# Block 0 of an FNet-plus-MLP kernel: centred rows go into its first product, and the tokens' scale is multiplied onto that product's sums

## The chip, the core and the metric

The kernel runs on one core of one Trainium2 chip. A core has five engines with a queue each: PE (TensorE, the matrix product), DVE (VectorE), ACT (ScalarE), POOL (GpSimd) and SP (SyncE, which here only starts transfers). Each takes its instructions strictly in its own order and waits on semaphores of the others. The metric is the device time of one execution in microseconds (us).

## What is computed

x has 2048 tokens of 640 numbers, float32. Each token is normalized over its 640 numbers, and three things are added up:

```
xn  = (x - mean(x)) / sqrt(var(x) + 1e-5)          # per token
A   = Real(DFT_tokens(DFT_hidden(xn)))              # by products with given cos/sin matrices
B   = gelu(xn @ w1 + b1) @ w2 + b2                  # 640 -> 1536 -> 640
out = x + A + B
```

The change touches the start of B. The normalization is two steps per token: subtract the mean ("centre") and multiply by one number r = 1/sqrt(var + 1e-5). As r belongs to a token and not to one of the 640 numbers, (x - mean) * r @ w1 is the same as r * ((x - mean) @ w1).

## The kernel before

**Tiles.** The tokens are worked in four blocks of 512. In a block, w1's 1536 columns are 12 units of 128. `hidden(g)` makes unit g's 128 x 512 sums in one bank of the accumulator: 15 matmuls of 128 x 512 (five slices of the 640 numbers, three matmuls each, because each operand is split into a high part, rounded to the type float32r in which the matmuls run, and a low remainder, and high*high, high*low and low*high are added). `gelu` copies the sums through the activation (`unit`), and splits the result into high (`high`, on ACT) and low (`low`, on DVE, source minus high). `output(i)` is another 15 matmuls with w2. `prep_w1` and `prep_w2` split the weights of a unit in the same manner, the high part on ACT, the low one on DVE. So the third matmul of each `hidden` needs a DVE result.

**Start.** Block 0's four row tiles (128 tokens each) are loaded, the PE is kept busy with `NWARM` matmuls on zeros, the rows are normalized into `xp`, turned with 20 PE transposes into five banks, and split from there into XT. The first loads of w1 go into the buffers that the warming matmuls read, so load 0 waits for the first `NGATE[0]` of these.

**Loop.** After units 0 and 1 comes `for i in range(10)`: split w1 of unit i+3 and w2 of unit i+1, run `hidden(i+2)`, its `gelu`, then `output(i)`. The order of each engine's work is the order of the program text; nothing reorders it. Woven into it are the jobs of `background(i)` (ahead of `hidden`) and `late(i)` (behind `gelu`): blocks 1 ("a", tokens 512 to 1023) and 2 ("b", tokens 1024 to 1535) are loaded, their statistics taken (`ln_stats`), they are normalized in place, and copied by DMA into another layout, `put_z`: `Z["b"]` (z_b in the profile, from the rows `r`) and `Z["a"]` (named row in the profile, from the rows `rt`); 16 transfers of 80 KB each, b's half on POOL's and half on SP's queue, a's all on POOL's. `put_rows` writes normalized rows to a scratch tensor `xn`. From z_b and z_a, `make_forms` makes transposed and split operands that the next stage needs: a DVE transpose into one of two buffers, then high on ACT and low on DVE. Forms b (vb0, vb1, ob0) are made in `background(4)`, forms a (ua0, ua1, va0, then an addition onto z_b) in `background(6)`.

The functions and lines that matter below: `split`/`high`/`low` L176 to L189, `load_x` L208, `ln_stats` L215, `ln_scale` L222, `ln_apply` L231, `transpose_z` L259, `load_w1` L278, `product` L300 to L302, `hidden` L320, `unit` L340, `add` L463, the warming matmuls L666, `transpose_x` L682, block 0's normalization L690 to L734, `put_z` L762, `put_rows` L770.

## Time and profile before

| what | value |
|---|---|
| runs shown | 851.45, 851.50 and 852.02 us, median 851.5 |
| profiled execution: span from first to last instruction | 849.9 us |
| its own time | not listed; the runs' median is 1.6 us above the span |
| PE busy | 841.9 us, 99% of the span |
| DVE, ACT, POOL busy | 686.7, 368.6, 67.7 us |
| DMA | 166.5 MB, mean 196 GB/s |

In the rows of a timeline stand the start in us from the span's start, the length, the engine, the line, the operation, what is written and read by the program's names, the shape and count, and in brackets how long the engine stood idle before and what ended that. "x15" is a merged run of 15 instructions. The profile's names drop buffer numbers: `ab` is a unit's activation, `hs` its split, `xab`, `as` and `w1f` are places of split w1 (and later of forms), `xc`, `r`, `rt` of split w2. In the rows of a tile's view stand line, engine, operation, count, shortest/median/longest in ns, and first and last start in us.

### The profile page before, as it was taken

The numbers are of one execution on the slowest core, as the hardware profiler recorded it, in microseconds if no ns is written. First come the engines' busy times: TensorE is split into PE (matmuls) and PEld (weight loads), VectorE is DVE, ScalarE is ACT, GpSimd is POOL, SyncE is SP. The second block draws the span as 40 slices with busy tenths as digits, with TensorE's granted clock in tenths as the row PEclk, the third lists the DMA queues.
The fourth block names the chain that finished last, engine by engine and source line by source line (L and its number), as shares of the span: only waits on it lengthen the run. The fifth ranks groups of instructions, "written<-read, shape, count | busy, mean of one in ns | idle before, by whom it ended". The sixth has DMA issues, their size and how long they took to land.

```text
span 849.9 us, 10599 instructions
## 1 busy us (share of the span) xinstructions
PE 841.9 (99%) x3711; PEld 696.7 (82%) x3711; DVE 686.7 (81%) x909; ACT 368.6 (43%) x527; POOL 67.7 (8%) x116
## 2 busy tenths in 40 slices
PE   8999999999999999999999999999999999999997
PEld 7888888888888888888888888888888888888886
DVE  7979889767844778979978887889967998885687
ACT  7655666654453555443444344232323433323241
POOL 0440024222301000000000000000000000000002
PEclk9999999999999999999999999999999999999999
DMA  8995667878977897958744679763745799705464
GB/s 230 288 248 158 139 163 250 260 223 305 262 192 199 333 323 138 209 120 193 158 137 107 167 220 283 165 144 99 214 150 156 229 237 234 303 19 180 124 172 108
DMA packets 199141, 166.53 MB, mean 196 GB/s; under 512 B 61648, under 2 KB 170192, under 8 KB 198576
## 3 DMA queue, kind: packets, MB, share of 16 engines
q1 hardware_dynamic: 188320, 140.42, 62.7%
q0 software_dynamic: 7600, 24.91, 8.7%
q10 hardware_dynamic: 3168, 0.52, 0.3%
q8 instruction: 29, 0.48, 0.2%
q14 instruction: 24, 0.20, 0.1%
HBM read 115.75 MB, written 46.14 MB: 190 GB/s over the span
## 4 chain that ended last, share of the span: by engine, by line
PE 98%; DMA 1%; DVE 0%; ACT 0%; SPq 0%; issue 0%; ACTq 0%
PE banks L301 29%; PE banks L302 29%; PE banks L300 29%; PE banks L320 10%; DMA row<-in_A_x_dram 1%; PE banks L682 0%; DVE st L215 0%; ACT xp L714 0%; SPq L208 0%; DVE yo L1722 0%; DVE mv L216 0%; ACT mv L707 0%; DVE mv L708 0%; ACTq L707 0%
## 5 line engine op out<-in xcount | busy, mean ns | idle before, releaser
L186 ACT ACTIVATE as<-r 128x1024 fp32r<-128x1024 f32 x80 | 85.0, 1062 | 171.1 <-PE banks L302 150.4
L300 PE MATMUL banks<-as,xab 128*128 128x512 f32 x407 | 158.3, 389 | 0.0
L302 PE MATMUL banks<-as,xab 128*128 128x512 f32 x407 | 158.3, 389 | 0.0
L301 PE MATMUL banks<-as,xab 128*128 128x512 f32 x407 | 158.3, 389 | 0.0
L189 DVE TENSOR_TENSOR as<-r,as 128x1024 fp32r<-128x1024 f32 x80 | 97.2, 1215 | 38.1 <-ACT as L186 38.0
L301 PEld LDWEIGHTS banks<-as,xab 128*128 128x128 f32 x407 | 76.4, 188 | 15.9
L302 PEld LDWEIGHTS banks<-as,xab 128*128 128x128 f32 x407 | 76.4, 188 | 15.8
L300 PEld LDWEIGHTS banks<-as,xab 128*128 128x128 f32 x407 | 76.4, 188 | 15.8
L300 PE MATMUL banks<-as,xc 128*128 128x512 f32 x224 | 87.1, 389 | 0.0
L301 PE MATMUL banks<-as,xc 128*128 128x512 f32 x224 | 87.1, 389 | 0.0
L302 PE MATMUL banks<-as,xc 128*128 128x512 f32 x224 | 87.1, 389 | 0.0
L186 ACT ACTIVATE as<-rt 128x1024 fp32r<-128x1024 f32 x32 | 34.0, 1063 | 72.5 <-PE banks L302 57.9
L320 PE MATMUL banks<-xt,xab 128*128 128x512 f32 x240 | 56.8, 390 | 0.0
L189 DVE TENSOR_TENSOR hs<-ab,hs 128x512 fp32r<-128x512 f32 x36 | 24.7, 685 | 37.6 <-ACT hs L186 37.6
L320 PEld LDWEIGHTS banks<-xt,xab 128*128 128x128 f32 x240 | 45.0, 188 | 9.4
L301 PEld LDWEIGHTS banks<-as,xc 128*128 128x128 f32 x224 | 42.1, 188 | 8.8
L302 PEld LDWEIGHTS banks<-as,xc 128*128 128x128 f32 x224 | 42.0, 188 | 8.7
L300 PEld LDWEIGHTS banks<-as,xc 128*128 128x128 f32 x224 | 42.1, 188 | 8.7
L1280 POOL DMA_DIRECT2D out_dram<-u x4 | 2.6, 658 | 568.8 <-DVE u L463 568.8
L302 PE MATMUL banks<-hs,xc 128*128 128x512 f32 x120 | 46.7, 389 | 0.0
L300 PE MATMUL banks<-hs,xc 128*128 128x512 f32 x120 | 46.7, 389 | 0.0
L301 PE MATMUL banks<-hs,xc 128*128 128x512 f32 x120 | 46.7, 389 | 0.0
(240 smaller groups left out, 1678.9 us busy)
## 6 DMA issues: line engine op xcount, KB each, us to landing
raw<-in_A_dft_seq_re_dram SPq DMA_DIRECT2D x64, 256.0 KB, 5.4
raw<-in_A_dft_seq_im_dram SPq DMA_DIRECT2D x64, 256.0 KB, 5.1
w1r<-in_B_w_dram SPq DMA_DIRECT2D x144, 80.0 KB, 3.5
wit<-wst POOLq DMA_DIRECT2D x15, 384.0 KB, 4.2
wit<-wst POOLq DMA_DIRECT2D x20, 256.0 KB, 4.5
forms_ab<-xab SPq DMA_DIRECT2D x4, 1280.0 KB, 7.7
xab<-wit SPq DMA_DIRECT2D x13, 384.0 KB, 4.5
row<-xn SPq DMA_DIRECT2D x14, 320.0 KB, 5.3
```

The costliest lines, as they stand in the source:

```text
L186: nc.scalar.activation(h, s, AF.Copy)
L189: nc.vector.tensor_tensor(l, s, h.bitcast(F32), op=ALU.subtract)
L300: nc.tensor.matmul(acc, wh, mh, start=first, stop=False, skip_group_check=goes_on)
L301: nc.tensor.matmul(acc, wh, ml, start=False, stop=False, skip_group_check=goes_on)
L302: nc.tensor.matmul(acc, wl, mh, start=False, stop=last, skip_group_check=goes_on)
L320: nc.tensor.matmul(acc, W1[i][:, a, j * P : (j + 1) * P], XT[j][:, b], start=n == 0, stop=n == len(steps) - 1)
L1280: queues[q % len(queues)].dma_start(rows_of(out, t)[:, :, q * DQ + c0 : q * DQ + c1], src[q * B : (q + 1) * B])
```

## The change

1. **Start.** Rows 0 to 3 are only centred, not scaled (`centre` on DVE, `centre_beside` on ACT): rows 0 and 2 and most of 3 on DVE, row 1 and two slices of row 3 on ACT. Variances of rows 1 and 3 come from a squared sum on ACT (`spread_beside`), row 3's only after XT is split. The high part of w1's unit 0 moves from ACT to DVE. The order of unit 0's matmuls (`FIRST`) changes a little, its last one runs amid unit 1's. 14 warming matmuls instead of 19; the first load of w1 waits for 6 of them instead of 7.
2. **Scale.** r of the 512 tokens is computed after the split of XT (square root on ACT, four small steps on DVE), spread over 128 partitions by four PE transposes amid `hidden(1)`, and copied into `scale`. Each of the 12 units of block 0 gets one more DVE instruction: sums times `scale` (128 x 512), ahead of its activation.
3. **Rows of block 0** are no longer normalized in place on DVE (four instructions, L231) but on ACT from `xp` (`rows_beside(0)`).
4. **Blocks 1 and 2.** Block 2's rows are normalized on ACT (`ln_apply_beside`) at step 1; block 1 gets its own table of statistics `MVA`, its statistics and its normalization move to step 2 (they were taken at step 2 and ended at step 3), on DVE. Square roots are issued ahead of a unit's activation (`roots`), with an extra small square root before them.
5. **Order.** The low parts of the weights (DVE) are issued after the unit's multiplication, inside `gelu`. Forms b move from `background(4)`, ahead of `hidden(6)`'s activation, to `late(3)`, behind `hidden(5)`'s: in DVE's order they stood behind w1's unit 7, and stand ahead of it now, with unit 6's multiplication in between. Forms a move from step 6 to step 5: they stood behind w1's unit 9 and stand ahead of it now, with unit 8's multiplication in between. From step 4 on `background` runs behind `gelu`. The transfers of each queue keep their order.

```diff
-NWARM = 19
-NGATE = (7, 10)
+NWARM = 14
+NGATE = (6, 9)
...
-        low(l, s, h)
+        if rest is None:
+            low(l, s, h)
+        else:
+            rest.append(lambda: low(l, s, h))
...
-        m = MV[:, :n]
-        ve, r, t = m[:, :, 2], m[:, :, 3], m[:, :, 4]
-        nc.scalar.activation(r, m[:, :, 1], AF.Sqrt, bias=eps[:, 0:1])
-        nc.vector.tensor_scalar(ve, m[:, :, 1], EPS, None, op0=ALU.add)
+    def roots(m):
+        nc.scalar.activation(m[:, :, 3], m[:, :, 1], AF.Sqrt, bias=eps[:, 0:1])
...
+        m = (MVA if 4 <= c < 8 else MV)[:, slot[c]]
         eng.tensor_scalar(xt[c], xt[c], m[:, 0:1], m[:, 3:4], op0=ALU.subtract, op1=ALU.mult)
+    def ln_shift():
+        nc.vector.scalar_tensor_tensor(MV[:, :, 5], MV[:, :, 0], -1.0, MV[:, :, 3], op0=ALU.mult, op1=ALU.mult)
+    def ln_apply_beside(c):
+        m = (MVA if 4 <= c < 8 else MV)[:, slot[c]]
+        nc.scalar.activation(xt[c], xt[c], AF.Identity, bias=m[:, 5:6], scale=m[:, 3:4])
...
             acc = a
+        if g < NF:
+            add(a, acc, scale, ALU.mult)
+            acc = a
         nc.scalar.activation(a, acc, AF.Gelu_apprx_tanh, bias=b1c[:, i : i + 1])
...
-    FIRST = [(0, 0), (0, 2), (1, 0), (1, 2), (0, 1), (2, 0), (2, 2), (1, 1), (3, 0), (3, 2)]
-    FIRST += [(2, 1), (4, 0), (4, 2), (3, 1), (4, 1)]
+    FIRST = [(0, 0), (1, 0), (0, 2), (1, 2), (2, 0), (2, 2), (0, 1), (3, 0), (3, 2), (1, 1)]
+    FIRST += [(4, 0), (4, 2), (2, 1), (3, 1), (4, 1)]
...
-    last = 1
-    f, m = MV[:, 0], MV[:, last]
...
+    def centre(c, j0=0, j1=ND):
+        nc.vector.tensor_scalar(
+            chunked(xp[:, c])[:, :, j0:j1],
+            xt[c].rearrange("p (q c i) -> p q c i", q=Q, i=B)[:, :, j0:j1],
+            MV[:, c, 0:1],
+            None,
+            op0=ALU.subtract,
+        )
+    def centre_beside(c, j0=0, j1=ND):
+        nc.scalar.activation(
+            chunked(xp[:, c])[:, :, j0:j1],
+            xt[c].rearrange("p (q c i) -> p q c i", q=Q, i=B)[:, :, j0:j1],
+            AF.Identity,
+            bias=MV[:, c, 5:6],
+        )
+    scratch = mr.tile([P, 2 * TB], F32, tag="hs", bufs=3, name="scratch")[:, :D]
+    def mean_beside(c):
+        nc.scalar.activation(scratch, xt[c], AF.Copy, scale=-1.0 / D, accum_out=MV[:, c, 5:6])
+    def spread_beside(c):
+        nc.scalar.activation(scratch, xp[:, c], AF.Square, scale=D**-0.5, accum_out=MV[:, c, 1:2])
-    nc.scalar.activation(W1[0][:, 0], first_w1, AF.Copy)
+    centre(0)
+    mean_beside(1)
+    centre_beside(1)
+    spread_beside(1)
+    ln_stats(2)
+    centre(2, 0, 2)
+    mean_beside(3)
+    centre(2, 2, ND)
+    nc.vector.tensor_scalar(MV[:, 3, 0:1], MV[:, 3, 5:6], -1.0, None, op0=ALU.mult)
+    centre_beside(3, 0, 2)
+    centre(3, 2, ND)
     transpose_x(0, 0, ND)
+    transpose_x(1, 0, ND)
     transpose_x(2, 0, 2)
     transpose_x(3, 0, 2)
-    transpose_x(last, 0, ND)
     transpose_x(2, 2, ND)
-    transpose_x(3, 2, ND - 1)
+    transpose_x(3, 2, ND)
+    W1[0], first_w1 = slots[1, 0], w1r.pop(0).rearrange("p a b -> p (a b)")
+    nc.vector.tensor_copy(W1[0][:, 0], first_w1)
     nc.vector.tensor_tensor(W1[0][:, 1], first_w1, W1[0][:, 0].bitcast(F32), op=ALU.subtract)
     for j in range(ND):
         split(XT[j][:, 0], XT[j][:, 1], tacc[j])
-        if j == 0:
-            hidden(0, slice(0, 1))
-            transpose_x(3, ND - 1, ND)
...
     A["rows_a"] = rows_in("rt2")
     for c in range(NC, 2 * NC):
         load_x(c, home=A["rows_a"])
-    acc0 = hidden(0, slice(1, None))
+    acc0 = hidden(0, slice(0, 14))
     prep_w1(1)
-    acc1 = hidden(1)
+    spread_beside(3)
+    v, r, t = MV[:, :, 1], MV[:, :, 3], MV[:, :, 4]
+    nc.scalar.activation(r, v, AF.Sqrt, bias=eps[:, 0:1])
+    nc.vector.reciprocal(r, r)
+    nc.vector.scalar_tensor_tensor(t, r, -0.5, r, op0=ALU.mult, op1=ALU.mult)
+    nc.vector.scalar_tensor_tensor(t, v, EPS, t, op0=ALU.add, op1=ALU.mult)
+    nc.vector.scalar_tensor_tensor(r, t, 1.5, r, op0=ALU.add, op1=ALU.mult)
+    prep_w1(2)
     prep_w2(0)
-    prep_w1(2)
+    acc1 = hidden(1, slice(0, 2))
+    hidden(0, slice(14, None))
+    hidden(1, slice(2, 6))
+    for c in range(NC):
+        nc.tensor.transpose(bank(0)[:, c * P : (c + 1) * P], MV[:, c, 3:4].to_broadcast([P, P]), ident)
+    hidden(1, slice(6, None))
+    scale = rows.tile([P, TB], F32, tag="yt", bufs=2, name="scale")
+    nc.scalar.activation(scale, bank(0), AF.Copy)
     load_w2(3)
     load_w1(5)
...
                 xn[:, t * B : (t + 1) * B].rearrange("(c a) r d -> a r c d", a=NC)[a], rows[a * B : (a + 1) * B]
             )
-    def background(i):
+    def rows_beside(i):
         if i == 0:
             for c in range(NC):
-                ln_apply(c)
+                nc.scalar.activation(
+                    row_places[:, c].rearrange("p (q c i) -> p q c i", q=Q, i=B),
+                    chunked(xp[:, c]),
+                    AF.Copy,
+                    scale=MV[:, c, 3:4],
+                )
             put_rows(0, row_places)
+        if i in (1, 2):
+            nc.scalar.activation(eps[:, 1:2], eps[:, 0:1], AF.Sqrt)
+    def background(i):
+        if i == 0:
             ln_stats(8)
             ln_stats(9)
         if i == 1:
             ln_stats(11)
+            roots(MV)
         if i == 2:
-            ln_stats(4)
-            ln_stats(5)
-        if i == 4:
-            open_place(*PLACES[7])
-            new_forms(0, "vb", "ua", "va")
-            make_forms("b", "vb0", "vb1", "ob0")
-        if i == 6:
+            for c in range(NC, 2 * NC):
+                ln_stats(c)
+            roots(MVA)
+        if i == 5:
             put_rows(1, A["rows_a"], nc.sync)
             new_forms(3, "t1")
             make_forms("a", "ua0", "ua1", "va0")
-        if i >= 6:
+        if i >= 5:
             (ua, va), (ub, vb) = ((Z[k][:, :, : 2 * B], Z[k][:, :, 2 * B : 4 * B]) for k in "ab")
+        if i == 5:
+            add(ub, ub, ua, ALU.subtract)
         if i == 6:
-            add(ub, ub, ua, ALU.subtract)
-        if i == 7:
             make_forms("a", "oa0", "va1")
             open_place(*PLACES[8])
+        if i == 7:
             make_forms("b", "t10", "t11")
         if i == 8:
+            add(ua, vb, ua, ALU.subtract)
+            add(va, va, vb, ALU.subtract)
+        if i == 7:
             add(vb, vb, ub, ALU.subtract)
             turn_x("t20", "b")
             turn_x("t21", "b")
-            add(ua, vb, ua, ALU.subtract)
-            add(va, va, vb, ALU.subtract)
+        if i == 9:
             load_xo(0)
             for q in range(Q):
...
     def late(i):
+        if i == 3:
+            open_place(*PLACES[7])
+            new_forms(0, "vb", "ua", "va")
+            make_forms("b", "vb0", "vb1", "ob0")
         if i == 0:
             ln_stats(10)
+    def beside_split(i, lows):
         if i == 1:
-            ln_scale(NC)
+            ln_scale_table(MV)
+            ln_shift()
+        for f in lows:
+            f()
+        if i == 1:
             Z["b"] = zo_tile("z_b")
             for c in range(2 * NC, 3 * NC):
-                ln_apply(c)
+                ln_apply_beside(c)
             put_z(Z["b"], A["rows_b"], nc.gpsimd, nc.sync)
             put_rows(2, A["rows_b"])
         if i == 2:
-            ln_stats(6)
-            ln_stats(7)
-    def normalize_a():
-        ln_scale(NC)
-        Z["a"] = as_z(row_places)
-        for c in range(NC, 2 * NC):
-            ln_apply(c)
-        put_z(Z["a"], A["rows_a"], nc.gpsimd)
+            ln_scale_table(MVA)
+            Z["a"] = as_z(row_places)
+            for c in range(NC, 2 * NC):
+                ln_apply(c)
+            put_z(Z["a"], A["rows_a"], nc.gpsimd)
     XF = {}
...
             form(2)
-    gelu(0, acc0)
-    gelu(1, acc1)
+    a0 = unit(0, acc0)
+    a1 = mr.tile([P, TB], F32, tag="ab", bufs=2, name="ab1")
+    def second(k):
+        if k:
+            add(a1, acc1, scale, ALU.mult)
+    split_unit(0, a0, second)
+    nc.scalar.activation(a1, a1, AF.Gelu_apprx_tanh, bias=b1c[:, 1:2])
+    split_unit(1, a1)
     for i in range(NF - 2):
-        prep_w1(i + 3)
-        if i == 3:
-            normalize_a()
+        lows = []
+        prep_w1(i + 3, rest=lows)
         if i == NF - 3:
             new_pieces()
             make_pieces(0, "Ah", "Al")
-        prep_w2(i + 1)
+        prep_w2(i + 1, lows)
+        rows_beside(i)
+        if i < 4:
+            background(i)
+        acc = hidden(i + 2)
+        if i == NF - 3:
+            more_forms()
+        gelu(i + 2, acc, lambda k: beside_split(i, lows) if k else None)
         if i + 6 < NF + 3:
             load_w1(i + 6)
         load_w2(i + 4)
-        background(i)
-        acc = hidden(i + 2)
-        if i == NF - 3:
-            more_forms()
-        gelu(i + 2, acc)
+        if i >= 4:
+            background(i)
         late(i)
         output(i)
     prep_w2(NF - 1)
```

More of the change, by code (lines that the diff above doesn't have):

```diff
@@ L133 @@
     ident = early.tile([P, P], F32, name="ident")
+    MVA = early.tile([P, 4, 6], F32, name="mva")
     es_r = ExitStack()
@@ L174, in chunked, with split @@
         return ap.rearrange("p (c q i) -> p q c i", q=Q, i=B)
-    def split(hi, lo, src, perm=False):
+    def split(hi, lo, src, perm=False, rest=None):
         h, l, s = (hi, lo, src)
@@ L210, in ln_stats @@
     def ln_stats(c):
-        m = MV
+        m = MVA if 4 <= c < 8 else MV
         st = ST[c % 2]
@@ L682, in transpose_x @@
             nc.tensor.transpose(tacc[j][:, c * P : (c + 1) * P], xp[:, c, j * P : (j + 1) * P], ident)
-    last = 1
-    f, m = MV[:, 0], MV[:, last]
-    root, step, shift = f[:, 3:4], f[:, 4:5], f[:, 5:6]
-    ln_stats(0)
-    nc.scalar.activation(root, f[:, 1:2], AF.Sqrt, bias=eps[:, 0:1])
-    scratch = mr.tile([P, 2 * TB], F32, tag="hs", bufs=3, name="scratch")[:, :D]
-    nc.scalar.activation(scratch, xt[last], AF.Copy, scale=-1.0 / D, accum_out=m[:, 5:6])
-    nc.scalar.activation(
-        chunked(xp[:, last]),
-        xt[last].rearrange("p (q c i) -> p q c i", q=Q, i=B),
-        AF.Identity,
-        bias=m[:, 5:6],
-    )
@@ L699 @@
-    nc.scalar.activation(scratch, xp[:, last], AF.Square, scale=D**-0.5, accum_out=m[:, 1:2])
-    nc.vector.reciprocal(root, root)
-    nc.vector.scalar_tensor_tensor(step, root, -0.5, root, op0=ALU.mult, op1=ALU.mult)
-    nc.vector.scalar_tensor_tensor(step, f[:, 1:2], EPS, step, op0=ALU.add, op1=ALU.mult)
-    for c in (2, 3):
-        ln_stats(c)
-    others = MV[:, 1:NC]
-    v, r, t = others[:, :, 1], others[:, :, 3], others[:, :, 4]
-    nc.scalar.activation(r, v, AF.Sqrt, bias=eps[:, 0:1])
@@ L721 @@
-    nc.scalar.activation(xp[:, last], xp[:, last], AF.Copy, scale=m[:, 3:4])
-    W1[0], first_w1 = slots[1, 0], w1r.pop(0).rearrange("p a b -> p (a b)")
-    nc.scalar.activation(W1[0][:, 0], first_w1, AF.Copy)
-    for j0, j1 in ((0, 2), (2, ND)):
-        for c in (2, 3):
-            ln_apply_chunked(xp[:, c], c, j0, j1)
+    def centre(c, j0=0, j1=ND):
[6 more added lines that the diff above has]
+        )
@@ L1098, in between @@
         if p == 3:
-            ln_scale(NC)
+            roots(MV)
+            ln_scale_table(MV)
             Z["z"] = zo_tile("z3")
```

34 lines of the change are left out of this document (10 added, 24 removed).

## The prediction

> **What bounds the kernel now.** I read the page, the PE's waits, then each engine's timeline from 0 to 70 us.
>
> ```profile
> span 849.9 us, 10599 instructions
> PE 841.9 (99%) x3711; PEld 696.7 (82%) x3711; DVE 686.7 (81%) x909; ACT 368.6 (43%) x527; POOL 67.7 (8%) x116
> ```
>
> ```profile
> PE banks L666 <- DVE warm L657: 1.9, 1, 1.9
> PE banks L682 <- ACT xp L714: 0.7, 1, 0.7
> ```
>
> ```profile
> 1.92 7.05 PE L666 MATMUL banks<-warm 128*128 128x512 f32 x19 [1.92 <-DVE warm L657]
> 9.71 2.27 PE L682 MATMUL banks<-ident,xp 128*128 128x128 f32 x19 [0.73 <-ACT xp L714]
> 11.73 0.48 PE L320 MATMUL banks<-xt,xab 128*128 128x512 f32 x1
> 12.07 10.32 PE L320 MATMUL banks<-xt,xab 128*128 128x512 f32 x44
> 22.23 0.39 PE L300 MATMUL banks<-hs,xc 128*128 128x512 f32 x1
> 46.03 3.56 PE L320 MATMUL banks<-xt,xab 128*128 128x512 f32 x15
> ...
> 52.83 3.56 PE L320 MATMUL banks<-xt,xab 128*128 128x512 f32 x15
> ...
> 66.43 3.56 PE L320 MATMUL banks<-xt,as 128*128 128x512 f32 x15
> ```
>
> PE waits only in the first 10 us; from 12.07 on it never does. A step of the loop, 30 matmuls, takes 6.80 (from 46.03, hidden(6), to 52.83, hidden(7)), so one takes 0.227. So time is won only by an earlier first product, and lost wherever something behind it comes late. That PE never waits says nothing about margin; the other queues do.
>
> **The start.** What the change touches there:
>
> ```profile
> 3.73 0.89 DVE L215 BATCH_NORM_STATS2 st<-row 128x6 f32<-128x320 f32 x2 [1.20 <-DMA row<-in_A_x_dram]
> ...
> 6.23 0.89 DVE L215 BATCH_NORM_STATS2 st<-row 128x6 f32<-128x320 f32 x2 [0.46 <-DMA row<-in_A_x_dram]
> ...
> 11.83 3.07 DVE L189 TENSOR_TENSOR xt<-banks,xt 128x512 fp32r<-128x512 f32 x5
> ```
>
> ```profile
> 5.10 0.72 ACT L692 ACTIVATE scratch<-row 128x640 f32<-128x640 f32 x1
> ...
> 5.95 0.83 ACT L693 ACTIVATE xp<-row,mv 128x640 f32<-128x640 f32 x1
> 6.81 0.74 ACT L699 ACTIVATE scratch<-xp 128x640 f32<-128x640 f32 x1
> ...
> 8.66 0.90 ACT L714 ACTIVATE xp<-row,mv 128x640 f32<-128x640 f32 x1
> ...
> 11.03 2.56 ACT L186 ACTIVATE xt<-banks 128x512 fp32r<-128x512 f32 x5
> ```
>
> Five warming matmuls fewer, at the warm 0.23, end that run at 8.97 - 1.15 = 7.8. Row 0 is centred long before (statistics from 3.73, DVE), row 1 too. Row 3's chain is ACT's: mean of row 1 (0.85 to the next), centring (0.86), squares (0.93), mean of row 3 (0.85), two slices centred (about 0.4): 3.9 us from row 1's landing, which lies between 3.73 and 5.10; from 4.6 (my estimate) to 8.5. Twenty transposes at 0.12 (2.27/19) from 7.8 end at 10.1, row 3's first about 9.1. ACT's five splits follow each 0.51 (2.56/5) from 9.3; DVE's five lows each 0.61 (3.07/5) from 10.1, behind w1's parts. First product 10.0, one gap of 0.25 for the second split, 45 matmuls at 0.227 = 10.2, four added transposes 0.48: output(0) at 20.9 against 22.23. Gain 1.35; if row 1 lands at 3.73 or 5.10, 1.5 or 0.8. The new root and its DVE steps (0.93 + 0.3 on ACT, 4 x 0.2 on DVE) end near 14.8, as the PE reaches the added transposes at 15: bounds 0 and 0.5, taken as 0. Hidden(7) would begin at 52.83 - 1.35 = 51.5.
>
> **Steps 0 to 2.** Every unit gets a DVE multiplication from the accumulator, some 0.6 us like the lows from banks. DVE loses the rows of block 0 and of block 2, which ACT gains.
>
> ```profile
> 22.53 2.17 DVE L231 TENSOR_SCALAR row<-row,mv 128x640 f32<-128x640 f32 x4
> 24.62 0.88 DVE L215 BATCH_NORM_STATS2 st<-r 128x6 f32<-128x320 f32 x2
> ...
> 25.65 0.83 DVE L215 BATCH_NORM_STATS2 st<-r 128x6 f32<-128x320 f32 x2
> ```
>
> Units 0 and 1: the scale's copy ends near 16.2, the activation's load 17.5, activation, high and low of unit 0 follow by 19.6, and output(0) asks at 20.9: covered by 1.3. Step 0: ACT is through unit 1 at 20.2, splits two weights (1.4) and makes four rows of block 0 (0.8 each, by L693 and L714), to 24.8; DVE had them at 24.70 (22.53 + 2.17), so POOL's transfers of them start as before. They delay unit 2's activation to 24.8 and its high to 26.0, which output(2) needs only at 34.5. Step 1: DVE, from 26.0, has a low, two statistics (1.03 each, 24.62 to 25.65), a multiplication, five small steps and then unit 4's w1 low, done near 31.3; hidden(4)'s third matmul is due at 31.5. Step 2: a weight low (w2), unit 3's low, four statistics (4.1), a multiplication and unit 5's w1 low, near 38.1; due at 38.3. Margins of 0.2; I cost both at 0, with 0 to 1 as bounds. ACT pays two square-root loads and two activation loads, as many as before, plus two small roots at 0.2:
>
> ```profile
> 35.30 1.28 ACT L340 ACT_TABLE_LOAD   x1
> 36.60 0.69 ACT L340 ACTIVATE ab<-banks,b1c 128x512 f32<-128x512 f32 x1
> ```
>
> A switch costs 1.30 by these rows. The Trainium skill, "ScalarE: Activation LUTs", section "What ACT_TABLE_LOAD costs", adds a drain of about 1.38, 2.66 in all; here the next activation starts at once, so the trace does not agree. By it ACT, behind two switches, would have block 2 normalized 2.8 later, and z_b and the end of the kernel with it, near 856; I give that 0.01.
>
> **Forms b, where the sum is decided.**
>
> ```profile
> 33.05 2.18 DVE L231 TENSOR_SCALAR r<-r,mv 128x640 f32<-128x640 f32 x4
> ...
> 45.79 0.68 DVE L189 TENSOR_TENSOR hs<-ab,hs 128x512 fp32r<-128x512 f32 x1
> 46.39 0.81 DVE L189 TENSOR_TENSOR xab<-w1r,xab 128x640 fp32r<-128x640 f32 x1
> 47.12 0.82 DVE L189 TENSOR_TENSOR xc<-w2r,xc 128x640 fp32r<-128x640 f32 x1
> 49.94 1.30 DVE L259 STREAM_TRANSPOSE ztvb<-z_b 128x512 f32<-128x512 f32 x2 [2.00 <-DMA row<-rt]
> ...
> 53.49 0.69 DVE L189 TENSOR_TENSOR xab<-ztob,xab 128x512 fp32r<-128x512 f32 x1
> ...
> 62.69 1.30 DVE L259 STREAM_TRANSPOSE ztua<-row 128x512 f32<-128x512 f32 x2 [1.05 <-DMA row<-rt]
> ...
> 67.98 0.69 DVE L189 TENSOR_TENSOR hs<-ab,hs 128x512 fp32r<-128x512 f32 x1
> ```
>
> ```profile
> L762 POOL DMA_DIRECT2D z_b<-r x8: 552/552/553, 35.9 to 39.7; - x8
> L762 SPq DMA_DIRECT2D z_b<-r x8: 610/744/1512, 36.0 to 41.9; - x8
> ...
> DMA to landing us min/median/max: 3.5/4.3/7.4
> ```
>
> ```profile
> 25.00:36.00 11.00, 11.00 (x50) 9.13 (x49) 10.06 (x27) 6.34 (x9) 2.43 (x5) 1.00 0.96 303
> 36.00:50.00 14.00, 14.00 (x63) 11.58 (x63) 11.72 (x29) 8.61 (x12) 10.81 (x20) 1.00 0.96 264
> ```
>
> The column to read is the bracket: what DVE stood idle for. Before, DVE made unit 7's w1 low (46.39), needed at 53.28, and only then waited 2.00 us for z_b, whose last copy, issued at 41.9, lands about 41.9 + 7.4 = 49.3. Now forms b stand ahead of that low, in DVE's and in ACT's order. DVE comes to them near 45.3 (unit 5's multiplication at 43.1, after hidden(5); two weight lows; the unit's low) and stands still until z_b is there; behind it wait unit 6's multiplication, which hidden(6) has ready at 48.1, and the weights of hidden(7). Is it there earlier? ACT normalizes block 2 by about 34.7 instead of 35.2 (33.05 + 2.18), and the loads start one warming matmul (0.4: 7.05 for 19 is 0.37 in the mean) sooner; but the DMA share is 0.96 from 25 to 50, so copies issued sooner mostly queue. I take 0.5: transposes at 49.45. Bounds: 50.5 (block 1's copies, now sooner on POOL's queue, crowd it by the same 0.5) and 48.3 (three times the lead). The value stands nearest the row, 49.94, less what the two leads can give.
>
> From there: 3.55 to the last low (49.94 to 53.49), 0.6 for it, 0.6 for unit 6's multiplication, 0.82 for the w1 low: + 5.6 = 55.05. Hidden(7)'s third matmul would be at 51.5 + 0.45 = 51.95: PE stalls 3.1. Before it ran at 52.83 + 0.45 = 53.28, so the kernel is then 55.05 - 53.28 = 1.8 behind. Note that the start has cancelled out: z_b sets this moment, and a wait of PE before it, of up to 3.1, is swallowed too.
>
> **Forms a** (step 5) are likewise made ahead of unit 9's w1 low. If z_a lands as before, transposes at 62.69, next instruction 5.29 later (67.98), multiplication and low 1.4: 69.4, against 66.43 + 0.45 + 1.8 = 68.7, a loss of 0.7. Its copies are normalized some 3 us sooner, but queue behind the same POOL transfers; 0.6 to 1.5 sooner leaves 0.1 to nothing. I take 0.1. SP's list of transfers is the same; of its loads those whose buffer is freed by a later low (w1 of units 10 and 11) start 1 to 2 us later, and are needed a step or more after they land; 0. In steps 6 to 9 DVE has 0.6 more per step, of 6.8, and ends each within it; in the later stages PE is behind the old clock, so their margin has grown by what was lost; 0 for both, with 0 to 0.5 as bounds.
>
> Sum: 849.9 + 1.8 + 0.1 = 851.8 for the span; the runs' median is 1.6 above it (851.5): **853.4 us**, 0.22% slower.
>
> **Rivals.** A: z_b is in time, and the start's gain stays: 851.5 - 1.35 = 850.1, faster by 0.16%. It needs transposes by 51.95 - 5.6 = 46.3, 3.6 sooner than the row; they decide for faster from 47.65, 2.3 sooner. For it: POOL's half of z_b is issued by 39.7. Against it: the saturated share, and SP's last copy at 41.9. 0.20 with partial gains (851 to 852.5).
>
> B: DMA is more crowded, z_b at 50 to 50.5 and z_a unchanged: 2.5 to 3.2 slower, 854.0 to 854.7. For it: block 1's copies are issued into the same full queues. 0.17.
>
> C: PE's clock falls during the stall, 2.1 us idle, two matmuls, 0.9 idle. At the start 19 warming matmuls took 7.05 instead of 19 x 0.227 = 4.3: warming again costs up to 2.7, 856.1. The one gap in the trace (0.73 at 9.71) cooled nothing: the 44 after it ran at full rate. 0.07. The Trainium skill, "TensorE: Matmul & The Clock Gate", section "Part 1: The HAM clock gate", says half rate follows an idle window of about 3.4 us; by that rule this stall just escapes, and no run here shows such a gap yet.
>
> D: the start gains nothing. Then 853.4 all the same, by the cancelling.
>
> **How the numbers follow.** My case 0.55, its own range 852.6 to 854.2. The range 850.0 to 855.2 takes in A and B, and leaves out C, the slow drain and A's far end, 0.14. The measurement tells about 0.2% (1.7 us): slower means above 853.2, faster below 849.8. Slower: two thirds of 0.55, most of B, C: 0.59. Faster: A with a larger start gain, 0.07. The rest, 0.34, is the same.
>
> **What the changed profile would show.** L331 starting near 10.0; output(0) near 20.9; DVE's first transposes of z_b with a wait of about 4 us and a start near 49.4; unit 7's w1 low after them; PE waiting 2 to 3.5 us for ACT and DVE `xab` (w1) near 51.5 to 55, and little else. It is wrong if z_b lands before 47, or if PE waits somewhere I counted as covered: in hidden(4) or hidden(5), or beside the added transposes.

## The result and the profile after

The changed kernel takes 854.87 us (median of five runs, 853.0 to 855.65) against 851.59 for the kernel before: a ratio of 1.0037, 95% interval 1.0025 to 1.0049. It is slower, by 3.3 us. The profiled execution is the longest of its five, 855.65 with a span of 853.7, which is 3.8 above the span of 849.9 before. The page's first lines and PE's waits:

```profile
span 853.7 us, 10603 instructions
PE 843.9 (99%) x3710; PEld 697.1 (82%) x3710; DVE 688.5 (81%) x905; ACT 375.7 (44%) x538; POOL 67.6 (8%) x116
```

```profile
PE banks L680 <- DVE warm L671: 1.9, 1, 1.9
PE banks L331 <- ACT xab L190: 1.9, 1, 1.9
PE banks L331 <- DVE xab L193: 0.6, 1, 0.6
```

Two waits are new, both for w1 (`xab`), both at one place in PE's timeline:

```profile
10.21 5.34 PE L331 MATMUL banks<-xt,xab 128*128 128x512 f32 x21
...
45.09 3.56 PE L331 MATMUL banks<-xt,xab 128*128 128x512 f32 x15
...
53.97 0.73 PE L331 MATMUL banks<-xt,xab 128*128 128x512 f32 x2 [1.91 <-ACT xab L190]
55.31 4.83 PE L331 MATMUL banks<-xt,xab 128*128 128x512 f32 x13 [0.61 <-DVE xab L193]
...
63.38 3.56 PE L331 MATMUL banks<-xt,as 128*128 128x512 f32 x15
```

These five rows hold the whole difference. The first product starts at 10.21. Hidden(6) at 45.09 is 0.94 ahead of before (46.03). The third matmul of hidden(7), at 55.31, is 2.03 behind (53.28). Its 13 matmuls then take 4.83, where 13 at 0.227 and the last one's tail take 3.1, so hidden(8) at 63.38 is 3.75 behind (59.63). From there to the end nothing is added. The windows view says what the 4.83 were (the column behind POOL is the granted clock, then the DMA share):

```profile
51.90:55.30 3.40, 0.89 (x3) 0.30 (x2) 3.28 (x6) 2.35 (x4) 1.92 (x4) 1.00 1.11 252
55.30:58.70 3.40, 3.39 (x8) 2.68 (x9) 1.38 (x2) 1.72 (x3) 0.00 (x0) 0.53 1.11 245
58.70:60.10 1.40, 1.40 (x7) 1.12 (x6) 0.00 (x0) 0.74 (x1) 0.00 (x0) 0.93 1.12 239
```

Behind the stall PE ran 3.4 us at about half its clock: eight matmuls 0.427 apart, which is 1.6 of the 1.7 us lost there. Now what the stall waited for, on DVE and on ACT:

```profile
49.68 1.30 DVE L270 STREAM_TRANSPOSE ztvb<-z_b 128x512 f32<-128x512 f32 x2 [4.69 <-DMA w1r<-in_B_w_dram]
...
53.23 0.69 DVE L193 TENSOR_TENSOR xab<-ztob,xab 128x512 fp32r<-128x512 f32 x1
53.84 0.68 DVE L477 TENSOR_TENSOR ab<-banks,scale 128x512 f32<-128x512 f32 x1
54.44 0.81 DVE L193 TENSOR_TENSOR xab<-w1r,xab 128x640 fp32r<-128x640 f32 x1
```

```profile
50.43 1.22 ACT L190 ACTIVATE xab<-ztvb 128x512 fp32r<-128x512 f32 x2 [6.16 <-DVE ztvb L270]
52.57 0.63 ACT L190 ACTIVATE xab<-ztob 128x512 fp32r<-128x512 f32 x1 [0.92 <-DVE ztob L270]
53.18 0.74 ACT L190 ACTIVATE xab<-w1r 128x640 fp32r<-128x640 f32 x1
```

Forms b hold both engines from z_b's arrival (its last transfer landed at 49.36, the transposes start at 49.68; the bracket names a load of w1, but what the transposes read is z_b) until 53.2, and w1's unit 7 follows. So far this is the picture forecast. But the trace's landing times show a second thing: the last quarter of unit 7's load landed at 53.10, and before at 38.8. ACT reached it at 53.18, so this row shows no wait. The reason stands in the timelines of SP's queue, first of the kernel before, then of the changed one:

```profile
33.64 1.81 SPq L278 DMA_DIRECT2D w1r<-in_B_w_dram  x4
35.55 0.38 SPq L285 DMA_DIRECT2D w2r<-in_B_w_dram  x1
36.04 7.37 SPq L762 DMA_DIRECT2D z_b<-r  x8
43.51 6.16 SPq L278 DMA_DIRECT2D w1r<-in_B_w_dram  x4
```

```profile
31.18 0.95 SPq L296 DMA_DIRECT2D w2r<-in_B_w_dram  x1
35.09 7.49 SPq L784 DMA_DIRECT2D z_b<-r  x8
42.68 6.37 SPq L289 DMA_DIRECT2D w1r<-in_B_w_dram  x4
49.15 0.45 SPq L296 DMA_DIRECT2D w2r<-in_B_w_dram  x1
```

The loads of w1's unit 7 and w2's unit 5 stood ahead of z_b's eight transfers and now stand behind them. As the low parts of the weights moved into `gelu`, the loads that reuse their buffers moved behind `gelu` too, and the transfers of z_b are issued inside it. The description of the change above says that the transfers of each queue keep their order; for SP's queue that is wrong. While SP waits for block 2's normalization there is also little left to transfer (DMA share, second figure from the right; before, then after):

```profile
34.00:36.50 2.50, 2.50 (x12) 2.06 (x11) 2.50 (x5) 2.48 (x3) 0.60 (x2) 1.00 0.84 226
```

```profile
34.00:36.50 2.50, 2.50 (x13) 2.07 (x12) 2.40 (x9) 2.48 (x5) 1.14 (x3) 1.00 0.22 60
```

### The profile page after: what moved, and what is told of

Its sections match the earlier page's. It is cut to its first block, busy times and chain, and to the rows that moved or that the text cites. A ratio compares the mean times of both kernels' runs of the same rounds, so it can differ in the third digit from the quotient of the medians.

```text
span 853.7 us, 10603 instructions
## 1 busy us (share of the span) xinstructions
PE 843.9 (99%) x3710; PEld 697.1 (82%) x3710; DVE 688.5 (81%) x905; ACT 375.7 (44%) x538; POOL 67.6 (8%) x116
## 3 DMA queue, kind: packets, MB, share of 16 engines
q1 hardware_dynamic: 188320, 140.42, 62.5%
## 4 chain that ended last, share of the span: by engine, by line
PE 95%; ACT 2%; DMA 1%; DVE 1%; issue 1%; SPq 0%; ACTq 0%; DVEq 0%
PE banks L311 29%; PE banks L313 29%; PE banks L312 29%; PE banks L331 8%; PE banks L680 1%; DMA w1r<-in_B_w_dram 1%; ACT xab L190 0%; ACT r L242 0%; DMA z_b<-r 0%; SPq L784 0%; ACT row L800 0%; DVE xab L193 0%; PE banks L696 0%; ACT ab L354 0%; ACT L354 0%
## 5 line engine op out<-in xcount | busy, mean ns | idle before, releaser
L331 PE MATMUL banks<-xt,xab 128*128 128x512 f32 x240 | 59.2, 400 | 2.5 <-ACT xab L190 1.9
```

What stands on the lines that cost most here:

```text
L331: nc.tensor.matmul(acc, W1[i][:, a, j * P : (j + 1) * P], XT[j][:, b], start=n == 0, stop=n == len(steps) - 1)
```

## The experiments

The median, the range and the ratio to the kernel before (with its interval), all of runs on the same chip as the kernel before they are divided by:

| run | what is changed | median us (runs) | range | ratio |
|---|---|---|---|---|
| e1 | after, PE kept busy in the stall | 854.65 (5) | 854.07 to 856.42 | 1.0041 (1.0029 to 1.0053) |
| e2 | after, ten of z_b's transfers on POOL | 857.74 (5) | 855.62 to 858.59 | 1.0069 (1.0057 to 1.0082) |
| e3 | after, forms b behind unit 7 | 855.57 (5) | 854.77 to 856.48 | 1.0046 (1.0034 to 1.0058) |
| e4 | after, 19 warming matmuls | 856.10 (6) | 854.62 to 858.40 | 1.0053 (1.0042 to 1.0065) |
| e5 | after, loads ahead of z_b on SP | 856.58 (6) | 853.54 to 858.70 | 1.0057 (1.0042 to 1.0071) |
| e6 | e3 and e5 together | 853.78 (12) | 851.76 to 856.92 | 1.0028 (1.0015 to 1.0041) |
| e7 | before, loads behind z_b on SP | 854.12 (5) | 853.70 to 855.48 | 1.0033 (1.0021 to 1.0045) |
| e8 | before, forms b ahead of unit 7 | 853.72 (9) | 852.63 to 855.71 | 1.0027 (1.0017 to 1.0036) |
| e9 | e6, and forms a behind unit 9 | 853.12 (11) | 852.52 to 853.71 | 1.0019 (1.0010 to 1.0028) |
| e10 | e9, w1's first load 0.43 later | 852.99 (11) | 852.70 to 853.59 | 1.0017 (1.0008 to 1.0026) |
| e11 | before, forms a ahead of unit 9 | 851.97 (11) | 851.32 to 855.17 | 1.0007 (0.9998 to 1.0016) |
| e12 | e9, two subtractions on POOL | 852.97 (11) | 852.25 to 853.26 | 1.0016 (1.0007 to 1.0025) |

The theory at first was the forecast's: z_b sets the moment at which hidden(7) goes on, and the stall lowers the clock. The first four runs were made for it and its rivals, before SP's order was seen.

**e1: is the half rate a matter of PE's idleness?**

```diff
         for n, (j, k) in list(enumerate(steps))[part]:
             a, b = kinds[k]
+            if g == 7 and n in (0, 2):
+                for _ in range(8 if n == 0 else 3):
+                    nc.tensor.matmul(bank(5 + 8 % 3), W1[6][:, 0, :P], XT[0][:, 0], start=True, stop=True)
```

> The changed kernel with eleven additional matmuls whose result is not used: eight between output(4) and hidden(7), three between the second and the third matmul of hidden(7), all in time in which PE stood idle. Theory 1 (the stall of PE also lowers its clock): the third matmul of hidden(7) stays near 55.3, because DVE's low of w1 is not sooner, but the matmuls behind it run 0.227 apart at once, not 0.427; hidden(8) starts near 61.7 instead of 63.38, span about 852.1 against 853.7, time about 853.2, and the runs lie within 0.5 of each other instead of 2.6. Rival 1 (they ran slowly because their operands, or the data paths, were busy with DVE, ACT and the transfers): 0.427 again, 854.9, spread as before. Rival 2 (the fillers themselves delay hidden(7)): 855.5 or more.

PE's timeline and a window of e1:

```profile
54.29 0.73 PE L334 MATMUL banks<-xt,xab 128*128 128x512 f32 x2 [0.85 <-ACT xab L190]
...
55.56 3.11 PE L334 MATMUL banks<-xt,xab 128*128 128x512 f32 x13
61.90 3.56 PE L334 MATMUL banks<-xt,as 128*128 128x512 f32 x15
```

```profile
55.50:58.70 3.20, 3.20 (x15) 2.64 (x15) 1.52 (x2) 1.99 (x3) 0.00 (x0) 1.00 1.11 252
```

The trace answers as theory 1 said: the third matmul stays (55.56), the 13 take 3.11 instead of 4.83, the clock is 1.00, hidden(8) starts at 61.90. So it is PE's idleness that lowers the clock, not the other work there. The time does not follow: 854.65 and a range of 2.4, where 853.2 and 0.5 were expected. Two places hold the difference in the profile, which is the longest of the five: PE, now sooner, loses 0.5 at hidden(9) and 1.7 near 240, where it waits for ACT and DVE behind a load of w1 for which ACT waits 2.9 us. Three of the five runs (spans 852.2 to 852.6) lie near the span of 852.1 expected, two at 854.4.

**e2: z_b sooner.**

```diff
-                engines[q % len(engines)].dma_start(
+                (nc.gpsimd if a == 3 else engines[q % len(engines)]).dma_start(
```

> The changed kernel with ten instead of eight of z_b's sixteen transfers on POOL's queue, and six on SP's; nothing else is moved. In the trace of the changed kernel SP's sixth transfer of z_b landed at 45.7 and its last, issued at 40.6, at 49.4. Theory 1 (z_b's landing sets the moment at which hidden(7) goes on): z_b is complete near 46 to 46.5, DVE's transposes start there and not at 49.7, w1's low of unit 7 ends before PE needs it (52.3), no stall and no fall of the clock; the start's gain of 0.9 shows, less up to 0.5 at hidden(9): span 849.0 to 849.5, time 850.6 to 851.2. Rival (the transfers are limited by the DMA engines in all, whichever queue issues them): z_b at 48.5 or later, stall of 2.5 or more, time above 853.5.

z_b landed at 43.4, even sooner than expected, and forms b were done by 48.9. The theory fell all the same. ACT's timeline, then DVE's, then PE's:

```profile
47.59 0.63 ACT L190 ACTIVATE xab<-ztob 128x512 fp32r<-128x512 f32 x1 [0.91 <-DVE ztob L270]
50.83 0.74 ACT L190 ACTIVATE xab<-w1r 128x640 fp32r<-128x640 f32 x1 [2.61 <-DMA w1r<-in_B_w_dram]
```

```profile
44.70 1.31 DVE L270 STREAM_TRANSPOSE ztvb<-z_b 128x512 f32<-128x512 f32 x2
...
62.70 1.30 DVE L270 STREAM_TRANSPOSE ztua<-row 128x512 f32<-128x512 f32 x2 [1.72 <-DMA row<-rt]
```

```profile
66.90 0.73 PE L331 MATMUL banks<-xt,as 128*128 128x512 f32 x2 [0.99 <-ACT as L190]
69.46 4.63 PE L331 MATMUL banks<-xt,as 128*128 128x512 f32 x13 [1.83 <-DVE as L193]
```

With z_b out of the way, ACT waits for the load of w1's unit 7: this row made SP's order visible. And z_a, now at 62.5 instead of 59.7, holds up unit 9 in the same manner as z_b held up unit 7: PE stands idle 2.8 us at hidden(9), and its clock falls again, some 1.5 us after it goes on (the windows of e2):

```profile
69.40:71.00 1.60, 1.54 (x7) 1.28 (x8) 1.60 (x4) 0.67 (x2) 0.00 (x0) 1.00 0.62 170
71.00:72.70 1.70, 1.70 (x6) 1.32 (x5) 1.60 (x3) 1.22 (x3) 0.00 (x0) 0.50 0.72 167
```

**e3: forms b back behind unit 7** (from `late(3)` to step 4, behind `gelu`).

```diff
     def late(i):
-        if i == 3:
-            open_place(*PLACES[7])
-            new_forms(0, "vb", "ua", "va")
-            make_forms("b", "vb0", "vb1", "ob0")
...
     def background(i):
+        if i == 4:
+            open_place(*PLACES[7])
+            new_forms(0, "vb", "ua", "va")
+            make_forms("b", "vb0", "vb1", "ob0")
```

> The changed kernel with forms b made one stage later (step 4 behind hidden(6)'s split, not step 3), so that in DVE's and ACT's order they stand behind w1's unit 7. Theory 1: PE does not wait at hidden(7); forms a, ahead of w1's unit 9, now wait for z_a until 59.7 and cost up to 0.5 at hidden(9); span 849.0 to 849.5, time 850.6 to 851.2. Rival (DVE has too much work with one multiplication more per unit, wherever the forms stand): a stall of 2 or more at another unit, time above 852.5.

Neither: 855.57, no better than with forms b ahead. ACT now has nothing in front of unit 7, and waits for its load alone:

```profile
51.66 0.74 ACT L190 ACTIVATE xab<-w1r 128x640 fp32r<-128x640 f32 x1 [7.95 <-DMA w1r<-in_B_w_dram]
```

PE's listed waits at hidden(7), (8) and (9) come to 2.8 us. The third matmul of hidden(7) comes at 53.31, sooner than the changed kernel's 55.31, but still 1.5 behind PE's own pace (hidden(6)'s third matmul and the 6.80 of a step).

**e4: the old number of warming matmuls** (`NWARM = 19`, `NGATE = (7, 10)`).

> The changed kernel with the 19 warming matmuls of before (and their order of loads). The first product comes later by about 1.1. Theory 1 (z_b sets the moment, and the stall's length decides whether the clock falls): hidden(7) is reached about 1.1 later, its third matmul stays near 55.3, the idle time is about 1.1 shorter, and the clock does not fall: time about 853.2, less than the changed kernel's in spite of the later start. Rival 1 (clock falls all the same): 854.9, the start costs nothing. Rival 2 (the start adds to the time): 856.0.

Rival 2 was right: 856.1, though the interval of its ratio still overlaps the changed kernel's. In the profile, the longest of the six runs, the first product came at 11.11, z_b at 49.3 as ever, but unit 7's load at 55.8. PE's timeline:

```profile
56.69 6.11 PE L331 MATMUL banks<-xt,xab 128*128 128x512 f32 x15 [3.76 <-ACT xab L190]
```

So in this execution unit 7's load sets the moment and not z_b, and the later start is not swallowed.

**e5 and e6: loads first; loads first with forms b back.** From here theory 2 says that there are two causes of about equal size.

```diff
         for f in lows:
             f()
+        if i + 6 < NF + 3:
+            load_w1(i + 6)
+        load_w2(i + 4)
         if i == 1:
             Z["b"] = zo_tile("z_b")
...
         gelu(i + 2, acc, lambda k: beside_split(i, lows) if k else None)
-        if i + 6 < NF + 3:
-            load_w1(i + 6)
-        load_w2(i + 4)
```

> The changed kernel with the loads of w1 (unit i+6) and w2 (unit i+4) issued right behind the lows of the weights, so that those of w1's unit 7 and w2's unit 5 stand ahead of z_b's eight transfers on SP's queue, as before the change, and not behind them. Forms b stay ahead of w1's unit 7. Theory 2 (two causes of equal size: SP's order makes w1's unit 7 land at 53 instead of 39, and forms b hold ACT and DVE until 53): w1's unit 7 lands near 39 again, but forms b still wait for z_b until about 49.5; third matmul of hidden(7) near 55.1, no wait at hidden(8) and (9); time 853.0 to 855.0, the upper end if the clock falls. Theory 3 (SP's order is all of it, because z_b comes early enough once DMA is less behind): no stall, 850.6 to 851.2.

> The changed kernel with both put back: loads of w1 and w2 ahead of z_b's transfers on SP, and forms b behind w1's unit 7. Theories 2 and 3: no wait at hidden(7) or (8); at hidden(9) up to 0.5 for z_a; the start's gain stays: 850.6 to 851.2, faster than the kernel before by 0.4 to 1.0. Rival (DMA is saturated from 14 to 70 us, so a start 1 us sooner only meets late transfers somewhere else): PE waits at hidden(8) to (10) again, 851.6 or more.

In e5 unit 7 landed at 39.9, and the stall is the same as in the changed kernel, now by forms b alone (DVE's timeline, then PE's):

```profile
49.93 1.30 DVE L270 STREAM_TRANSPOSE ztvb<-z_b 128x512 f32<-128x512 f32 x2 [4.83 <-DMA row<-rt]
```

```profile
54.12 0.73 PE L331 MATMUL banks<-xt,xab 128*128 128x512 f32 x2 [1.93 <-ACT xab L190]
55.56 4.84 PE L331 MATMUL banks<-xt,xab 128*128 128x512 f32 x13 [0.70 <-DVE xab L193]
```

Theory 3 is out. The median, 856.58, lies above theory 2's upper end. e3 and e5 each take away one cause, and neither is faster than the changed kernel; e6 takes away both, and the only waits of PE listed in its profile (span 849.6) are in the first 11 us. But only five of its twelve runs look like that (851.8 to 852.2); the other seven lie between 853.2 and 856.9. So the two causes are real and there is something else. In the five of them above 855.5 the mean clock was 0.995 to 0.997. It is 0.998 or more in every run of the kernel before, whose profile has half rate only in the last 3.1 us, when PE has nothing left to do. So in these five the clock fell in mid kernel, as behind the stalls above.

**e7 and e8: each cause alone in the kernel before.** In e7 the loads of step 1 stand behind `late(1)`, in e8 forms b move from `background(4)` to `late(3)`.

```diff
-        if i + 6 < NF + 3:
-            load_w1(i + 6)
-        load_w2(i + 4)
+        if i != 1:
+            if i + 6 < NF + 3:
+                load_w1(i + 6)
+            load_w2(i + 4)
...
         late(i)
+        if i == 1:
+            load_w1(i + 6)
+            load_w2(i + 4)
```

> The kernel before with one change: the loads of w1's unit 7 and w2's unit 5 (step 1) are issued behind z_b's eight transfers on SP's queue. Theories 2 and 3: w1's unit 7 lands near 52 instead of 38.8; its high and low need 1.6 more, PE's third matmul of hidden(7), at 53.28 before, comes 0.5 to 1.5 later; w1's units 8 and 9 are late behind it; time 852.5 to 854. Rival (the order of forms b is all of it): 851.6, w1's unit 7 still in time.

> The kernel before with one change: forms b are made one step sooner, ahead of w1's unit 7 in DVE's and ACT's order. Theory 2: DVE and ACT wait for z_b until 49.4 and make w1's unit 7 behind the forms: low ends 49.9 + 3.55 + 0.6 + 0.8 = 54.9, third matmul of hidden(7) 1.6 later than 53.28, time 853.2. Theory 3: 851.6 to 852.0.

Both cost time: 2.4 and 2.0 us in the median, against a kernel without the new start, scale or ACT work. e7's ACT shows the reason in one row:

```profile
53.41 0.74 ACT L186 ACTIVATE xab<-w1r 128x640 fp32r<-128x640 f32 x1 [8.35 <-DMA w1r<-in_B_w_dram]
```

e8's profiled execution is its shortest; z_b came at 48.3 there, and its span is only 0.7 above that of before.

**e9, e10, e11: the third place.** z_a landed between 59.6 and 64.5 in the profiles so far. In e9 ua0, ua1, va0 and the addition stand in step 6 instead of 5, and oa0, va1 and the forms after them (but not t10, t11) a step later; e10 is e9 with `NGATE = (7, 9)`; e11 is the kernel before with ua0, ua1, va0 a step sooner.

```diff
-        if i == 5:
+        if i == 6:
             put_rows(1, A["rows_a"], nc.sync)
             new_forms(3, "t1")
             make_forms("a", "ua0", "ua1", "va0")
...
-        if i == 6:
+        if i == 7:
             make_forms("a", "oa0", "va1")
```

> As the run before with SP's loads and forms b put back, and forms a too: ua0, ua1, va0 and the addition behind w1's unit 9 (step 6), the forms after them a step later, as before the change. What stays of the change is the start, the scale with its multiplication per unit, and the normalization on ACT. Theory 4 (three places where a late transfer reaches PE: w1's unit 7 by SP's order, z_b by forms b, z_a by forms a; z_a landed between 59.6 and 64.5 in the profiles so far): no run is held by z_a, all runs lie within 1.5 us, median 850.6 to 851.2, faster than before by about the start's gain, 0.5 to 1.0. Rival (the spread of 851.8 to 856.9 comes from something else, such as the earlier loads of block 1 or the work moved onto ACT): again a median of 853 or more with single runs at 855 to 857.

> The same with w1's first load waiting for seven warming matmuls instead of six, that is issued 0.43 later. In the changed kernel row 3 of block 0 landed at 7.68 (7.04 before), after that load had begun, and DVE and ACT waited 0.6 to 0.7 for it. If the load crowds row 3: row 3 lands near 7.1 and the first product starts near 9.8 instead of 10.2 to 10.5; time 0.3 to 0.5 less than the kernel it is compared with. If not: no difference.

> The kernel before with one change: forms a (ua0, ua1, va0) are made one step sooner, ahead of w1's unit 9 in DVE's and ACT's order. Theory 4: DVE and ACT wait for z_a (62.6 in the profile before); w1's unit 9 is made behind it, its low done near 62.7 + 4.2 + 0.8 = 67.7 to 68.8, due 66.9: 0.8 to 2 lost, more where z_a is later or the clock falls; median 852.5 to 854, single runs to 856. Rival (forms a cost nothing by themselves): 851.6.

e9 has theory 4's spread and not its median: eleven runs within 1.2 us, where e6 spread over 5.2, but 853.12. PE no longer waits for a late transfer in the profile, and something costs more than the start had given. PE's timeline and the stretch from 62 to 104, of e9 and of the kernel before (the DVE column is the third time):

```profile
104.41 0.47 PE L311 MATMUL banks<-as,w1f 128*128 128x512 f32 x1 [1.51 <-ACT v L354]
```

```profile
62.00:104.00 42.00, 40.82 (x178) 32.80 (x176) 39.60 (x61) 24.37 (x40) 0.00 (x0) 1.00 0.56 137
```

```profile
62.00:104.00 42.00, 42.00 (x187) 34.79 (x186) 37.23 (x56) 24.70 (x41) 0.57 (x1) 1.00 0.64 149
```

Until 74 e9's PE is 1.67 ahead of before, at 108 it is 0.68 behind. DVE is busy 39.6 of the 42 us, 2.4 more than before; 1.8 of it are the multiplications of units 9 to 11, each 0.60 from its start to the next instruction's. e10 differs from e9 in time by nothing that can be told: row 3 landed at 7.14 as expected, but the first product came at 10.34, not 9.8. Its profile shows one thing more. Its start is 0.87 later than e9's, and yet PE waits as long at the same place:

```profile
105.29 0.47 PE L311 MATMUL banks<-as,w1f 128*128 128x512 f32 x1 [1.51 <-DVE zc L477]
```

Between 74 and 108, e9 goes from 1.67 ahead of the kernel before to 0.68 behind, e10 from 0.80 ahead to 1.58 behind: 2.35 and 2.38 lost. So the loss does not hang on how early PE is. And e6's profile, with the same multiplications but forms a still a step sooner, loses nothing there (0.24 ahead at 74, 0.19 at 108). It goes with the order of e9, in which DVE has more to do behind 74 (busy 28.0 of the 30 us to 104, 27.1 in e6); that this is the cause is argued. e11 missed: 0.35 us, within the interval, with one run of eleven at 855.17. In the kernel before forms a have margin enough; they lose it only with PE sooner. That z_a is what spread e6's runs is argued from e9; no profile of such a run was taken.

**e12: DVE relieved by POOL.**

```diff
-            add(ua, vb, ua, ALU.subtract)
-            add(va, va, vb, ALU.subtract)
+            nc.gpsimd.tensor_tensor(ua, vb, ua, op=ALU.subtract)
+            nc.gpsimd.tensor_tensor(va, va, vb, op=ALU.subtract)
```

> The kernel with SP's loads, forms b and forms a put back, and in addition the two subtractions behind them (row and z_b, 128x1024, 1.18 and 1.21 us on DVE at 82.8 and 83.9) moved from DVE to POOL, which is idle from 62 to 104. Theory 5 (with the late transfers out of the way, DVE is the bound from 62 to 104: it is busy 39.6 of 42 us there, the multiplications take 2.4 more than before, and PE waits 1.9 at 104.4 for its last result): DVE is through 2.4 sooner, the wait at 104.4 goes, and the start's gain of 0.8 to 1.6 reaches the end: median 850.4 to 851.2, faster than the kernel before by 0.4 to 1.2. Rival (POOL's subtractions slow DVE down, or the wait at 104.4 has another cause): 852.5 to 853.5 as without it.

The rival was right: 852.97. DVE's timeline and POOL's:

```profile
83.26 1.62 DVE L193 TENSOR_TENSOR w1f<-w1r,w1f 128x640 fp32r<-128x640 f32 x1 [0.22 <-ACT w1f L190]
84.80 0.68 DVE L477 TENSOR_TENSOR ab<-banks,scale 128x512 f32<-128x512 f32 x1
85.40 2.42 DVE L193 TENSOR_TENSOR rt<-w2r,rt 128x640 fp32r<-128x640 f32 x1
```

```profile
81.78 2.41 POOL L842 TENSOR_TENSOR row<-z_b,row 128x1024 f32<-128x1024 f32 x1 [28.02 <-DVE z_b L477]
84.14 3.00 POOL L843 TENSOR_TENSOR row<-row,z_b 128x1024 f32<-128x1024 f32 x1
```

The two lows of weights that run beside POOL take 1.62 and 2.42 instead of the 0.81 of such a low elsewhere (54.44 in the changed kernel): 2.4 us more, about what DVE was relieved of. DVE is busy 40.1 of the 42 us, no less than in e9, and PE still waits 1.3 at 104.2. So this run leaves open whether a DVE with less to do would end that wait.

## Why the forecast was right, and where it was not

The forecast was 853.4 in a range of 850.0 to 855.2, slower most likely; measured 854.87. Its sign and range held, but its account of the cause was half the story. That the range held is in part luck: it left out the fall of the clock, and the clock fell, at 1.7 us instead of up to 2.7.

- **Start.** Forecast: first product 10.0, gain 1.35. Measured 10.21 and 0.94 in the profile. The term that was mis-sized is row 3's chain: row 3 landed at 7.68 instead of 7.04, and ACT had its first slices centred at 9.14, not 8.5. Row 3 does not set the first product alone. In e5 and e10 it landed at 6.99 and 7.14, and the first product came at 10.37 and 10.34: PE began its transposes only at 8.06 and 7.98 (7.90 in the changed kernel), as all 14 warming matmuls had run at half clock, 0.427 apart (in e10 row 1 was late as well, at 5.29). In the six other profiles with 14 of them the transposes began between 6.68 and 7.24. The other 0.2 of the gain went between the first product and output(0), 11.08 against 10.9. Gains at hidden(6) were 0.66 to 1.67 over all profiles with this start; the bounds given were 0.8 and 1.5.
- **Added transposes, steps 0 to 2, table loads.** No wait of PE at any of them, as costed. The margins at hidden(4) and (5), put at 0.2, were about 0.9: the low of unit 5 ended at 37.8, and was due at 38.7.
- **Forms b.** The numbers hit: transposes 49.68 (49.45 forecast), third matmul 55.31 (55.05). The order of forms b costs 2.0 by itself (e8), and with unit 7's load in time it makes the whole stall (e5). But that z_b alone "sets this moment" was wrong: with z_b at 43.4 (e2) and with the forms behind unit 7 (e3) the third matmul came at 52.48 and 53.31, still 0.4 and 1.5 behind PE's own pace, for unit 7's load landed only at 50.7 and 51.6; after it hidden(9), and in e3 hidden(8) too, lost time.
- **SP's list.** This is the step that failed: "SP's list of transfers is the same; of its loads those whose buffer is freed by a later low (w1 of units 10 and 11) start 1 to 2 us later ... 0". Unit 7's load went behind z_b's transfers and landed 14 us later, which costs 2.4 by itself (e7). The agreement of 55.05 with 55.31 is no proof of the mechanism: two causes end within 0.1 us of each other, at 53.1 and 53.2.
- **The cancelling (also rival D).** "The start has cancelled out" and "853.4 all the same" fell with e4, whose median is 1.2 above the changed kernel's. Unit 7's four loads were issued there at 42.7 to 49.0 (42.7 to 48.2 in the changed kernel) and the last landed 2.7 us later; why is not shown.
- **Rival C, given 0.07, happened.** A third term was missing from the sum: 1.7 us at half rate. The step that failed is the argument from the gap of 0.73 at 9.71, which "cooled nothing"; it says nothing of a gap three times as long. In the five runs of the changed kernel the shortest, 853.0, has the highest mean clock (0.998), the longest, 855.65, has 0.996: a difference of 0.002 is 1.7 us, so most of that spread may be the clock's. This is not shown: the profile of the kernel before has 0.998 too, from its last 3.1 us alone, in which PE is idle and half rate costs nothing.
- **Forms a** cost nothing in the changed kernel, for PE was 3.75 late by then (0.1 forecast). Behind a PE that is not late they cost from 0.4 us (e6's profile) to 2.8 us and a fall of the clock (e2).
- **Rival A** ("z_b is in time") was mispriced: with z_b in time at 43.4, e2 was slower, not 850.1. And with all three places mended (e9) 2.35 us are lost between 74 and 108. The forecast had costed DVE's added work in steps 6 to 9 at 0 with a bound of 0.5 ("DVE has 0.6 more per step, of 6.8, and ends each within it"). If that work is the cause, as argued, the bound was wrong for e9's order; the changed kernel, 3.75 late, could not show it.
- **Span to time.** The 1.6 added to the span was the median of the runs less the span of one execution. In the changed kernel's runs the time lies 1.9 to 2.0 above the span, in those runs of the kernel before that list both 1.8 to 2.1: 0.3 to 0.4 more.

The sum by the trace: start -0.94, stall +2.97, half rate +1.7, forms a 0: +3.75, against +1.9 forecast. None of these kernels is faster than the one before. Whether the start's gain can be kept, with less on DVE in the stretch from 62 to 104, stays open.

## What to carry to other kernels

When an edit moves the instruction that frees a buffer, the load that reuses the buffer moves with it, past everything that is issued in between on its queue: list each queue's transfers in order, before and after, and don't infer from the program text that they kept it. Where a calculated moment agrees with the trace, look whether another cause ends at the same moment; the test is to take each away alone, and then both. A gain at the start is only kept if what PE needs later comes early enough as well: here z_a's transfers did not (e2). And look at the next busiest engine before giving it more work (here DVE, 37 of 42 us busy before).

## What was not expected of the hardware

- PE's clock fell after an idle stretch that was neither long nor whole: in the changed kernel after 1.91 and 0.61 us with two matmuls between, in e2 after 0.99 and 1.83, and there only about 1.5 us after the matmuls had begun again. Single waits of 1.1 (e7) and 1.5 us (e9) did not lower it. In e4 a single wait of 3.76 did. When the clock fell can be read from the granted clock in narrow windows. It stayed at half for 3.41 us in the changed kernel, e2 and e5, and for 6.83, twice that, in e4; and the stretch at full rate ahead of each fall was 14, 19, 14 and 14 times 3.41. So cut each trace into stretches of 3.41 us from the moment at which its clock first rose. Here are e2's stretch ahead of the fall and e10's stretch with the wait of 1.51 (the second figure is PE's busy time):

```profile
67.59:71.00 3.41, 1.58 (x8) 1.28 (x8) 3.41 (x6) 1.36 (x2) 0.00 (x0) 1.00 0.78 235
```

```profile
103.44:106.85 3.41, 1.90 (x9) 1.33 (x8) 2.82 (x5) 2.07 (x4) 1.13 (x2) 1.00 0.83 129
```

Over all 14 profiles, their last microseconds included, the clock fell behind each such stretch in which PE was idle for 1.83 us or more, and behind none with 1.79 or less; behind one with 1.65 it stayed at half (e4). In the changed kernel the idle time in its stretch was 2.52. By these rows about half a stretch is enough (an estimate), and whether a given wait lowers the clock also depends on where a stretch begins. The Trainium skill, "TensorE: Matmul & The Clock Gate", section "Part 1: The HAM clock gate", puts half rate behind at least one idle window of about 3.4 us that runs freely of the program. The even multiples of 3.41 and the delay in e2 agree with a window of that length that runs freely; that the window must be idle throughout does not agree, since 1.83 us of idle time were enough in e2.
- POOL's elementwise work and DVE's exclude each other where both read two operands from SBUF (e12). The multiplication that reads the accumulator kept its 0.68 beside POOL, the lows with two operands in SBUF doubled or tripled. The Trainium skill, "SBUF — State Buffer", section "SBUF: two separate sides", says just this: a pair of ports shared by DVE and GpSimd, locked for a whole instruction. These rows agree.
